# First batch in two token parts, and the first four tiles of a fused attention and FFN kernel as one written program order

## Chip, cores and metric

One core of a Trainium2 chip; the experiments ran in sessions on two such chips. The metric is device microseconds of the whole program, median of several executions; all runs quoted are of the state "fast" but for one, which is named. A profile is one of those executions. TensorE is PE in the profile (PEld its weight loads), VectorE is DVE, ScalarE is ACT, GpSimd is POOL.

## The reference

```python
# q, k, v: [8 batches, 8 heads, 576, 64] float32; w_in [512, 2048], w_out [2048, 512]
scores = q @ k.T / 8
rel = i - j
mask_plain = (rel >= 0) & (rel < 32)                       # heads 0 to 3
mask_dil   = (rel >= 0) & (rel < 128) & (rel % 4 == 0)     # heads 4 to 7
x = softmax(where(mask, scores, -1e9)) @ v                 # -> [4608 tokens, 512]
h = maximum(x @ w_in, 0)
out = (h * h) @ w_out
```

## The kernel before

Tokens come in 8 batches of 576 and the FFN takes them in 9 tiles of 512. Attention of a batch is cut into steps, each with a letter, a head pair e (0 and 1 plain, 2 and 3 dilated) and a token part: `q k` (capital for part 1) transpose on TensorE and copy out of PSUM, `v V` spread the values, `a b` are the scores of part 0 and 1, `o p` the value product, its normalization (two ScalarE passes, `rec`) and the product `xT` that the FFN reads. A tile's FFN is 32 groups of matmuls; a step has the number of the group (slot) behind which it is emitted. The order of emission is the order in which the instructions of each engine stand in its queue.

```python
FIRST = "k0 q2 q0 q3 k3 k2 k1 a0 b0 q1 a2 a1 v2 b2 b1 o0 p0 a3 o1 v3 p1 o2 b3 p2 o3 p3".split()
EARLY = {   # batch: "slot:step ..."
    1: ("21:q1 23:k0 23:q2 25:k2 25:v2 26:q0 27:v3 27:a0 27:a2 28:k1 29:k3 29:o0 29:a1 29:Q1 29:q3 29:o2  "
        "29:o1 30:a3 30:Q0 31:K1 31:o3 32:K0 32:Q2 34:Q3 35:b0 37:b1 37:K2 37:K3 37:V2 39:p0 39:b2 39:V3  "
        "39:p1 40:b3 43:p3 43:p2"),
    2: (...),                      # cut: "8:q0 ... 31:p3", counted from tile 1
}
WHOLE = (0, 2, 3)                  # batches that are transposed in one piece; 1 in two token parts
w_cuts = (0, 512, 1024, 2048)      # pieces of w_in
# ... cut: pools, masks, loads, steps
ps_f: 4 PSUM buffers, ps_a: 2, ps_o: 1, ps_d: 1
# value product of a part (cut)
for x, (oo, i, rh) in enumerate(mms):
    nc.tensor.matmul(oo, vb[:, e, i, :], rh, ...)           # po
for x, (dd, rh) in enumerate(dms):
    nc.tensor.matmul(dd, ones[:, :], rh, ...)               # pd, the row sums
nc.scalar.activation(rec[:, 0:n], d[:, 0:n], ACT.Ln)
nc.scalar.activation(rec[:, 0:n], rec[:, 0:n], ACT.Exp, scale=-1.0)
nc.vector.tensor_tensor(out=tok, in0=o, in1=rec, op=ALU.mult)   # xT
# the end of the kernel (cut)
for x, code in enumerate(FIRST):
    step(0, code)                                           # all of batch 0 ahead of the FFN
for tk0, nt in [(0, NT), (NT, NT // 2), (NT + NT // 2, NT // 2)] + [(NT * t, NT) for t in range(2, NTILES)]:
    groups += ffn_groups(tk0, nt)                           # tile 0 whole, tile 1 in halves
for g, group in enumerate(groups):
    group()
    while steps and steps[0][0] <= g:
        step(*steps.pop(0)[1:])
```

The softmax here doesn't subtract the row's maximum and nothing guards it: scores larger than these inputs give would overflow.

Of the kernel before, what the change touches and what calls it, by code (L numbers as in the profile page):

```python
# [12 lines left out]
RES = 4  # L13

ORDER = (0, 2, 1, 3)

FIRST = "k0 q2 q0 q3 k3 k2 k1 a0 b0 q1 a2 a1 v2 b2 b1 o0 p0 a3 o1 v3 p1 o2 b3 p2 o3 p3".split()

EARLY = {
    1: (  # L20
        "21:q1 23:k0 23:q2 25:k2 25:v2 26:q0 27:v3 27:a0 27:a2 28:k1 29:k3 29:o0 29:a1 29:Q1 29:q3 29:o2  "
        "29:o1 30:a3 30:Q0 31:K1 31:o3 32:K0 32:Q2 34:Q3 35:b0 37:b1 37:K2 37:K3 37:V2 39:p0 39:b2 39:V3  "
        "39:p1 40:b3 43:p3 43:p2"
    ),
    2: (
        "8:q0 10:k0 12:q2 13:k1 14:v3 14:a0 14:v2 15:q1 16:b0 16:o0 16:k2 18:q3 20:p0 21:a1 22:b1 22:k3 22:a2  "
        "22:o1 24:b2 25:o2 27:p1 27:a3 28:p2 28:b3 29:o3 31:p3"
    ),
}


def _masks() -> np.ndarray:
# [23 lines left out]
def kernel(  # L56
# [9 lines left out]
    nc = tc.nc  # L66
    P = nc.NUM_PARTITIONS
    B, H, S, D = q.shape
# [15 lines left out]
    MN = (64, M - 64)  # L84
    NT = 512
    NTILES = NTOK // NT
    WHOLE = (0, 2, 3)
    RING = 4 * S
    KT = DM // P
    NF = DFF // P  # L90
# [21 lines left out]
    mask_d = const.tile([P, 256 + 512], bf16, name="mask_d")  # L112
    mask_h = const.tile([P, 2 * 176 + 64], bf16, name="mask_h")

    w_cuts = (0, 512, 1024, 2048)
    w_in_sb = [
        const.tile([P, KT, c1 - c0], bf16, name=f"w_in{c0}") for c0, c1 in zip(w_cuts, w_cuts[1:])
    ]
# [94 lines left out]
    def trans(b: int, e: int, nm: str, part: int):  # L213

        ps = ps_a.tile([P, 1024], bf16, name="pa")
        t = staged(b, nm)
        copy = nc.scalar.copy if nm == "q" and e < NE // 2 else nc.vector.tensor_copy
        if b == 0:

            pv_ = ps[:, 0:S].rearrange("p (r m) -> p r m", r=RES)  # L220
            for r in range(RES):
                for a in range(2):
                    for hl in range(2):
                        nc.tensor.transpose(
                            pv_[64 * hl : 64 * hl + 64, r, 72 * a : 72 * a + 72],
                            t[0:72, 2 * e + hl, a, D * r : D * r + D],
                            ident[0:72, 0:72],
                        )
            if nm == "q":
                copy(qT[:, e, :, :], pv_)  # L230
                return
            for hl in range(2):
                rows = slice(64 * hl, 64 * hl + 64)
                if e < NE // 2:
                    copy(
                        kbd[rows, e, :, rows].rearrange("p i (m r) -> p i m r", r=RES),
                        pv_[rows, :, :].rearrange("p r (i m) -> p i m r", i=NB),
                    )
                else:
                    copy(  # L240
                        kbd[rows, e, 0:8, rows].rearrange("p (x r) m -> p r x m", x=2),
                        pv_[rows, :, 0:128].rearrange("p r (x m) -> p r x m", x=2),
                    )
                    copy(
                        kbd[rows, e, 8, rows].rearrange("p (m r) -> p m r", r=RES),
                        pv_[rows, :, 128:M].rearrange("p r m -> p m r"),
                    )
            return
        if b in WHOLE:
            m0, n, pitch, cuts = 0, M, M, [(t[0:72, :, a, :], 72 * a, 72) for a in range(2)]  # L250
        else:

            m0, n, pitch, cuts = MS[part], MN[part], 80, [(t[0:80, part, :, :], 0, 80)]
        pv_ = ps[:, 0 : 4 * pitch].rearrange("p (h c m) -> p h c m", h=2, c=2)
        for hl in range(2):
            for c in range(2):
                for src, c0, w in cuts:
                    nc.tensor.transpose(  # L258
                        pv_[:, hl, c, c0 : c0 + w], src[:, 2 * e + hl, P * c : P * c + P], ident[0:w, 0:w]
                    )  # L260
        halves(e, nm, pv_[:, :, :, 0:n], m0, n, copy)
# [31 lines left out]
    def blocks(b: int, e: int, part: int):  # L293



        if e < NE // 2:
            if part == 0:
                return [(i, None, 16 * i, min(16 * i + 24, 64)) for i in range(4)]
            return [(3, None, 64, 72)] + [(i, None, 16 * i, min(16 * i + 24, M)) for i in range(4, NB)]  # L300
        if b != 1:
            rs = (2 * part, 2 * part + 1)
            return [x for r in rs for x in ((r, r, 0, 96), (4 + r, r, 64, M))] + [(8, None, 128, M)] * (part == 0)
        if part == 0:
            return [(r, r, 0, 64) for r in range(RES)]
        return [x for r in range(RES) for x in ((r, r, 64, 96), (4 + r, r, 64, M))] + [(8, None, 128, M)]

    def half_at(b: int, e: int):

        return (352, mask_p) if e < NE // 2 else (256, mask_d) if b == 1 else (416, mask_h)  # L310

    pts = {}

# [25 lines left out]
    def pv(b: int, e: int, part: int, spare=None, name=""):  # L339
# [6 lines left out]
            o = spare.tile([P, 512], f32, name=name)  # L346
            d = spare.tile([P, 512], f32, name=name)
        c = half_at(b, e)[0] * part
        byr = dil and b != 1
        mms, dms = [], []  # L350
        if byr:
            n = 2 * M
# [39 lines left out]
        tok = xT[:, e, t0 : t0 + S]  # L392
        if byr:
            tok = tok[:, n * part : n * part + n]
        elif b == 1:
            tok = tok[:, RES * MS[part] : RES * MS[part] + n]
        else:
            tok = tok.rearrange("p (r m) -> p r m", r=RES)[:, :, MS[part] : MS[part] + MN[part]]
            o, rec = o3, rec[:, 0:n].rearrange("p (r m) -> p r m", r=RES)
# [4 lines left out]
    def step(b: int, code: str):  # L404
# [8 lines left out]
        elif what in "qQkK":  # L413
            trans(b, e, what.lower(), part)
        elif what in "vV":
            spread_v(b, e, [part] if b == 1 else [0, 1])
        elif what in "ab":
            scores(b, e, part, *((ps_f, "pf") if b == 0 else ()))
        elif b == 0 and part:
            pv(b, e, part, ps_a, "pa")  # L420
        elif b == 1 and e % 2:
            pv(b, e, part, ps_f, "pf")
        else:
            pv(b, e, part)
# [11 lines left out]
    def store(osb, pos: int):  # L436

        x = 0
        while x < P:
            b, y = divmod(pos + x, S)  # L440
            part = int(y >= RES * MN[0]) if b == 1 else 0
            w = MN[part] if b == 1 else M
            r, m = divmod(y - RES * MS[part], w)
            n = min(P - x, w - m)
            row = b * S + RES * (MS[part] + m) + r
# [95 lines left out]
    put(md[:, :, 32:112], mk[:, 160:240].unsqueeze(1).broadcast_to([P, RES, 80]))  # L541
    put(mask_d[:, 704:768], mk[:, 96:160])

    load_qk(0, None, [0])
    load_qk(0, None, [2, 3])
    load_qk(0, None, [1])
    load_v(0, [0, 1], "0pr1")

    for x, (w, c0, c1) in enumerate(zip(w_in_sb, w_cuts, w_cuts[1:])):
        nc.gpsimd.dma_start(w[:, :, :], moe_w_in[:, c0:c1].rearrange("(kt p) f -> p kt f", p=P))  # L550
    for c in range(4):
        nc.gpsimd.dma_start(
            w_out_sb[:, 4 * c : 4 * c + 4, :].rearrange("p f m -> p (f m)"),
            moe_w_out[512 * c : 512 * c + 512, :].rearrange("(p f) m -> p (f m)", p=P),
        )

    for x, code in enumerate(FIRST):
        step(0, code)
        if x == 1:

            for nm in "qk":
                nc.vector.memset(staged(1, nm)[64:80, 0, :, :], 0.0)
    zero_halves(vbd[1])
    load_qk(1, 0, [0, 1, 2, 3])
    load_v(1, [0])
    load_qk(1, 1, [0, 1, 2, 3])
    load_v(1, [1])
    load_qk(2, None, [0, 1, 2, 3])
    G = 2 * NF

    LOAD_V = {2: 0, 3: G + 16, **{b: G * (b - 2) for b in range(4, B)}}
    CROSS = {4: 2 * G + 8, **{b: G * (b - 2) + 5 for b in range(5, B)}}
    LOAD_QK = {3: G + 14, 4: 2 * G - 8, 5: 3 * G - 5, **{b: G * (b - 3) + 6 for b in range(6, B)}}
    groups, steps = [], []
    for tk0, nt in [(0, NT), (NT, NT // 2), (NT + NT // 2, NT // 2)] + [(NT * t, NT) for t in range(2, NTILES)]:
        groups += ffn_groups(tk0, nt)
    for b, table in EARLY.items():
        for x in table.split():
            slot, code = x.split(":")
            steps.append((G * (b - 1) + int(slot), b, code))  # L580
    steps += attention_steps(
        3, 2 * G, {"q": (-7, 8), "k": (-5, 8), "v": (-7, 8), "a": (-1, 8), "b": (0, 8), "o": (3, 8), "p": (6, 8)}
    )
    for b in range(4, B):
        steps += attention_steps(
            b, G * (b - 1),
            {"k": (-9, 4), "q": (-9, 4), "v": (-7, 8), "a": (-1, 8), "b": (0, 8), "o": (3, 8), "p": (6, 8)},
        )
    steps.sort(key=lambda x: x[0])
    for g, group in enumerate(groups):  # L590
        t = g // G
        for b in [x for x in CROSS if CROSS[x] == g]:
            for part in range(2):
                for nm in "kq":
                    cross(b, nm, part)
        for b in [x for x in range(2, B) if LOAD_V[x] == g]:
            load_v(b, [0, 1])
        for b in [x for x in range(3, B) if LOAD_QK[x] == g]:
            for part in [None] if b in WHOLE else [0, 1]:
                load_qk(b, part, [0, 1, 2, 3])  # L600
        group()
        while steps and steps[0][0] <= g:
            step(*steps.pop(0)[1:])

# [29 lines left out]
```

## Time and profile before

| | before |
|---|---|
| median of executions | 329.8 us |
| TensorE busy | 304.7 of 329.3 us |
| first w_in matmul, first w_out matmul | 27.1, 42.1 us |
| tile 0 done, tile 1 done, tile 2 done | 61.6, 105.6, 139.6 us |
| last FFN matmul done | 324.9 us |

Read it as a relay: from the first w_in matmul on, TensorE should never lack work, and a steady tile takes 32.5 us. What the first three tiles take over that is where time can come from. The stretches quoted in the prediction show it; "tile done" is the start of the next tile's first w_in matmul in the timeline.

### The profile page before, as it was taken

How to read it: one execution, taken by the hardware profiler on the slowest of the kernel's cores; microseconds unless marked ns; L12 is line 12 of the kernel's file. 1: busy time of each engine (PE TensorE's matmuls, PEld its weight loads, DVE VectorE, ACT ScalarE, POOL GpSimd, SP SyncE). 2: the span in 40 equal slices, each digit the busy share in tenths (PEclk: the TensorE clock that was granted, in tenths of full speed). 3: DMA queues.
4: the chain of work that ended last, by engine and by line, in shares of the span. 5: the costliest groups of instructions: out<-in, count | busy, mean ns of one | idle time of the engine just before them, and what ended most of it. 6: DMA issues, size and time to landing. Idle time of an engine off the chain costs nothing.

```text
span 329.3 us, 6594 instructions
## 1 busy us (share of the span) xinstructions
PE 304.7 (93%) x2490; PEld 184.0 (56%) x2490; DVE 199.6 (61%) x610; ACT 196.0 (60%) x419; POOL 82.3 (25%) x125
## 2 busy tenths in 40 slices
PE   0489998989997999999999999999999999999994
PEld 0474544775964655555559955555555555445541
DVE  6586518799865876898389738972897214203400
ACT  5096734776876893488448844884488446416511
POOL 8662287245235014440144024000000000000000
PEclk9997999999999999999999999999999999999999
DMA  7999999989976976999279927191200120031021
GB/s 98 126 174 214 202 168 129 182 98 159 129 77 87 148 93 91 155 152 170 55 115 148 171 60 116 34 146 32 71 27 3 43 79 7 1 94 35 0 64 64
DMA packets 74079, 33.07 MB, mean 100 GB/s; under 512 B 44736, under 2 KB 68416, under 8 KB 74048
## 3 DMA queue, kind: packets, MB, share of 16 engines
q0 software_dynamic: 49296, 18.37, 49.1%
q1 hardware_dynamic: 24608, 14.16, 19.3%
q8 instruction: 19, 0.31, 0.4%
q10 hardware_dynamic: 144, 0.13, 0.1%
q14 instruction: 12, 0.10, 0.1%
HBM read 36.83 MB, written 9.44 MB: 141 GB/s over the span
## 4 chain that ended last, share of the span: by engine, by line
PE 72%; DVE 12%; ACT 8%; DMA 3%; issue 2%; POOL 1%; ACTq 0%; POOLq 0%
PE pf L499 35%; PE pf L471 27%; DVE kbd L275 4%; PE po L385 3%; DMA kb<-in_k_dram 3%; PE pd L387 2%; DVE h2T L483 2%; DVE qT L271 2%; DVE xT L400 2%; ACT rec L389 1%; ACT h2T L482 1%; ACT qT L271 1%; ACT pt L333 1%; ACT osb L505 1%; PE pa L329 1%
## 5 line engine op out<-in xcount | busy, mean ns | idle before, releaser
L471 PE MATMUL pf<-xT,w_in 128*128 128x512 bf16 (+1 forms) x704 | 135.4, 342 | 0.3 <-ACT osb L505 0.2
L499 PE MATMUL pf<-w_out_sb,h2T 128*128 128x512 bf16 x576 | 134.8, 379 | 0.0
L482 ACT ACTIVATE h2T<-pf 128x512 bf16<-128x512 f32 x144 | 83.9, 596 | 29.6 <-PE pf L471 28.3
L471 PEld LDWEIGHTS <-w_in 128*128 128x128 bf16 x704 | 74.9, 114 | 40.3 <-issue 2.1
L483 DVE TENSOR_TENSOR h2T<-h2T 128x512 bf16<-128x512 bf16 x144 | 58.2, 422 | 40.3 <-ACT h2T L482 39.2
L499 PEld LDWEIGHTS <-h2T 128*128 128x128 bf16 x576 | 52.1, 98 | 53.4
L400 DVE TENSOR_TENSOR xT<-po,rec 128x288 bf16<-128x288 f32 (+2 forms) x56 | 25.5, 456 | 43.2 <-ACT rec L390 42.2
L505 ACT COPY osb<-pf 128x512 f32<-128x512 f32 x36 | 21.1, 587 | 49.5 <-PE pf L499 45.2
L170 POOL DMA_DIRECT2D vbd<-in_v_dram x36 | 25.9, 732 | 57.2 <-PE pd L387 43.8
L389 ACT ACTIVATE rec<-pd 128x288 f32<-128x288 f32 (+2 forms) x56 | 23.0, 411 | 25.9 <-PE pd L387 25.0
L333 ACT ACTIVATE pt<-pa 128x352 bf16<-128x352 f32 (+4 forms) x56 | 27.9, 501 | 5.9 <-PE pa L323 4.5
L390 ACT ACTIVATE rec<-rec 128x256 f32<-128x256 f32 (+2 forms) x64 | 28.4, 443 | 2.0
L385 PEld LDWEIGHTS <-vbd 128*128 128x128 bf16 x326 | 20.4, 100 | 15.9 <-issue 6.8
L385 PE MATMUL po<-pt,vbd 128*128 128x32 bf16 (+3 forms) x281 | 19.6, 200 | 4.4 <-DVE xT L400 4.3
L183 POOL DMA_DIRECT2D vd<-in_v_dram x28 | 17.0, 630 | 10.2 <-DMA kb<-in_k_dram 5.0
L387 PE MATMUL pd<-pt,mk 128*128 128x96 bf16 (+4 forms) x220 | 19.5, 211 | 0.0
L275 DVE COPY kbd<-pa 64x288 bf16<-64x288 bf16 (+2 forms) x32 | 12.8, 399 | 6.7 <-PE pa L258 6.1
L271 DVE COPY qT<-qx 64x288 bf16<-64x288 bf16 x64 | 15.5, 242 | 1.4
L387 PEld LDWEIGHTS <-mk 128*128 128x128 bf16 x252 | 15.2, 100 | 0.6 <-issue 0.5
L323 PEld LDWEIGHTS <-kbd 128*128 128x128 bf16 x176 | 11.6, 101 | 6.6 <-DVE qT L271 0.9
L275 DVE COPY kbd<-kx 64x288 bf16<-64x288 bf16 x32 | 15.0, 470 | 0.3
L334 DVE TENSOR_TENSOR pt<-pt,mask_p 128x352 bf16<-128x352 bf16 (+1 forms) x32 | 11.7, 372 | 5.3 <-ACT pt L333 5.2
(58 smaller groups left out, 210.3 us busy)
## 6 DMA issues: line engine op xcount, KB each, us to landing
vd<-in_v_dram POOLq DMA_DIRECT2D x32, 64.0 KB, 4.5
w_out_sb<-in_moe_w_out_dram POOLq DMA_DIRECT2D x4, 512.0 KB, 17.2
vbd<-in_v_dram POOLq DMA_DIRECT2D x28, 72.0 KB, 5.1
out_dram<-osb SPq DMA_DIRECT2D x7, 256.0 KB, 3.0
qb<-in_q_dram POOLq DMA_DIRECT2D x5, 320.0 KB, 5.9
kb<-in_k_dram POOLq DMA_DIRECT2D x5, 320.0 KB, 6.0
out_dram<-osb SPq DMA_DIRECT2D x7, 224.0 KB, 2.3
out_dram<-osb SPq DMA_DIRECT2D x12, 128.0 KB, 3.7
```

Of the source, the lines that this page charges most:

```text
L170: nc.gpsimd.dma_start(dst[rows, e, i0:i1, rows], v[b, 2 * e + hl, 64 * i0 : 64 * i1, :].rearrange("(i p) d -> p i d", p=64),)
L275: copy(kbd[rows, e, m0 // 16 : (m0 + n) // 16, rows].rearrange("p i (m c j) -> p j i m c", c=2, j=2)[:, jj, :, :, :], src.rearrange("p c ( ...
L333: nc.scalar.activation(pt[:, off : off + n], ps[:, 0:n], ACT.Exp, scale=SCALE)
L385: nc.tensor.matmul(oo, vb[:, e, i, :], rh, start=(x == 0), stop=(x == len(mms) - 1), skip_group_check=True)
L387: nc.tensor.matmul(dd, ones[:, :], rh, start=(x == 0), stop=(x == len(dms) - 1), skip_group_check=True)
L389: nc.scalar.activation(rec[:, 0:n], d[:, 0:n], ACT.Ln)
L390: nc.scalar.activation(rec[:, 0:n], rec[:, 0:n], ACT.Exp, scale=-1.0)
L400: nc.vector.tensor_tensor(out=tok, in0=o if o is o3 else o[:, 0:n], in1=rec if o is o3 else rec[:, 0:n], op=ALU.mult)
L471: nc.tensor.matmul(acc[u][:, nt * x + y0 : nt * x + y1], w_in_sb[piece][:, kt, c0 : c0 + 509 : 4], xT[:, kt, t0 : t0 + y1 - y0], start=(kt ...
L482: nc.scalar.activation(hv, acc[u][:, :].rearrange("p (x n) -> p x n", x=per), ACT.Relu)
L483: nc.vector.tensor_tensor(out=hv, in0=hv, in1=hv, op=ALU.mult)
L499: nc.tensor.matmul(cur[m][:, :], h2[:, f, P * m : P * m + P], w_out_sb[:, f, :], start=(f == 0), stop=(f == NF - 1),)
```

## The change

Its intent: the first half tile needs only 256 tokens, so batch 0 is loaded and computed in two token parts, FFN begins after part 0, and both halves of tile 0 use the first half of w_in before the second half is needed. For the first four tiles one written program gives the order of loads, steps and groups. (Not shown below: some steps of batch 0 use other PSUM buffers, and the q and k steps of batch 5 move into the program.)

```diff
-WHOLE = (0, 2, 3)
+WHOLE = (2, 3)
+PARTED = (0, 1)
-w_cuts = (0, 512, 1024, 2048)
+w_cuts = (0, 1024, 2048)
-FIRST = ...   EARLY = ...
+PROGRAM = (   # "|" is an FFN group; "L" is a load: batch, what, part, heads; i/o are pieces of w_in/w_out
+    "L0:q023 L0:q00 L0:q01 0k0 L0:q10123 0q0 0q1 0k1 L0:v0pd 0a0 0q2 L0:i0 0a1 0k3 L0:v1dpr 0k2 0q3 0Q1 "
+    "0K3 0a3 0Q3 0K2 0a2 0v2 0Q0 L0:i1 L0:o2 0K0 0o0 0v3 0b0 0Q2 0o2 0K1 0b3 0o1 L0:o0 0o3 0V3 0b2 0b1 | "
+    "0V2 | 0p0 | 0p1 0p2 | L0:o1 0p3 L0:o3 | | | y | | | | | | | | L1:q00123 z | | | | | L1:v0dp "
+    "L1:q10123 | | L2:qw0123 L1:v1dpr 1q1 1q3 | 1q2 | 1k2 | 1k1 1v3 | 1a2 | 1v2 1k0 1q0 | 1o2 | 1a0 1a1 | "
+    "1k3 1o0 1o1 | 1a3 1Q0 | 1K0 1o3 | 1Q1 1K1 | 1Q2 | 1b0 | | 1Q3 1K2 L2:vwpdr | | | 2q0 | | 2k0 1V2 | "
+    "1b2 1p0 | 1b1 1V3 1K3 | | 1p2 1p1 | 2a0 1b3 | 2k1 2o0 2b0 1p3 | 2q1 2k2 | | ..."
+    # cut: to the end of tile 3
+)
-for tk0, nt in [(0, NT), (NT, NT // 2), (NT + NT // 2, NT // 2)] + ...
+for tk0, nt in [(NT // 2 * t, NT // 2) for t in range(4)] + ...
+head = groups[:G]
+groups[:G] = [x for y in (0, 16, 4, 20, 8, 12, 24, 28) for x in head[y : y + 4]]
```

## The prediction

> **What bounds the kernel now.** I read the busy table first, then the table by stretches, then the chain that ended last, then the timeline of the places where the chain leaves TensorE.
>
> ```profile
> PE 304.7 (93%) x2490; PEld 184.0 (56%) x2490; DVE 199.6 (61%) x610; ACT 196.0 (60%) x419; POOL 82.3 (25%) x125
> ...
> PEclk9997999999999999999999999999999999999999
> ```
>
> TensorE is busy 93%, at full clock but for one slice, the fourth. So the end is TensorE's work plus the time in which it lacked work. Cutting the span where one FFN tile of 512 tokens gives way to the next (the copies of the last output rows in the chain, and the first matmul of the next tile) shows where it lacked work:
>
> ```profile
> 0.00:27.20 27.20, 13.33 (x239) 11.98 (x240) 18.26 (x38) 14.55 (x37) 17.89 (x30) 0.97 1.11 140
> 27.20:61.60 34.40, 32.84 (x216) 16.92 (x213) 19.52 (x56) 19.19 (x47) 16.49 (x24) 0.97 1.24 179
> 61.60:105.50 43.90, 40.13 (x487) 30.89 (x483) 35.24 (x116) 30.96 (x71) 18.66 (x27) 1.00 0.98 118
> 105.50:139.60 34.10, 34.05 (x292) 19.38 (x290) 25.16 (x84) 22.36 (x50) 10.11 (x16) 1.00 0.84 119
> 139.60:172.10 32.50, 32.30 (x244) 17.88 (x241) 23.27 (x77) 21.15 (x45) 9.39 (x15) 1.00 0.89 124
> 172.10:204.70 32.60, 32.41 (x307) 24.59 (x304) 23.26 (x77) 21.14 (x46) 9.37 (x15) 1.00 0.92 125
> ```
>
> Columns after the stretch and its length: PE, PEld, DVE, ACT and POOL busy, clock, DMA share, GB/s. Rows are the start and tiles 0 to 4. The steady tile is 32.5 us. FFN work in one tile is 128 matmuls of 512 columns; the chain shows 64 of them in 13.81 us, so 27.6 us, which leaves 4.9 us for one batch's attention. Tile 2 takes 1.6 us more because its batch is also transposed on TensorE. Tile 1 takes 43.9 us. The start takes 27.2 us, and the first matmuls after it run at half clock:
>
> ```profile
> 26.77 0.48 PE pa L387 x3
> 27.25 4.50 PE pf L471 x16
> 31.78 10.52 PE pf L471 x48
> 42.30 5.18 PE pf L499 x24
> ```
>
> Sixteen matmuls cost 4.50 us there and 3.5 us at the rate of the next 48 (0.22 us each), so about 1.0 us is lost to the clock. Where tile 1 loses time:
>
> ```profile
> 100.28 0.33 PE L385 MATMUL po<-pt,vbd 128*128 128x96 bf16 x5 [0.69 <-DVE xT L400]
> 100.44 1.99 DVE L275 COPY kbd<-pa 64x288 bf16<-64x288 bf16 x4
> 102.46 0.46 DVE L400 TENSOR_TENSOR xT<-po,rec 128x288 bf16<-128x288 f32 x1
> 102.97 0.33 PE L385 MATMUL po<-pt,vbd 128*128 128x96 bf16 x5 [1.15 <-DVE xT L400]
> ```
>
> TensorE waits for an output normalization (xT) that stands behind four key copies of a later batch on VectorE, which was busy 35.24 of 43.9 us in this tile.
>
> **What the Trainium skill says.** *TensorE: Matmul & The Clock Gate*, "Part 1: The HAM clock gate": about 3.4 us of sustained work release a half-rate clock. The trace agrees in kind: granted clock 0.50 from 26 to 28 us, 0.69 from 28 to 30, then 1.00. An earlier FFN does not escape this, since the work before it stays sparse. The same page, "Architectural detail", calls ScalarE and VectorE strict FIFOs; the timeline above agrees, with the xT instruction behind the four copies. *DMA: Bandwidth & Descriptors*, "Specifications", asks for at least 512 B per transfer; from 12 to 14 us, 1557 of 1617 packets are below that and 112 GB/s move, against 211 GB/s for weights from 30 to 32 us. *Perfetto Trace Analysis*, "Tensor Engine Instruction", calls matmul ends estimated. So I count from start to start (512 columns: 216 ns, where the table of groups says 379).
>
> **The change, part by part.**
>
> *Two token parts for batch 0.* TensorE gets its transposes as 128 pieces of 64 or 80 tokens instead of 128 of 72: no gain or loss. What moves is the dependency. The first half tile (256 tokens) needs only part 0 of batch 0, so the four PV steps of part 1 go behind the first FFN groups. Now the start, by hand. In the trace about 1.15 MB of q and k are in by about 12 us, and part 1 of k is last in the new order too, so it lands at 12. From there VectorE has, in the order of the built program up to the last xT of part 0: four k copies for each of the two dilated pairs at part 1 (0.96 us a pair, from 0.27 and 0.21 us), two k copies for each plain pair (0.9), three q or mask items of about 0.3 early and three of about 0.4 late, two value spreads of 0.6, and four xT of 0.42. Sum: 1.9 + 1.8 + 0.9 + 1.2 + 1.2 + 1.7 = 8.7 us. With 0.8 us from landing to the first copy it ends near 21.5. ScalarE has about 6 us in the same stretch, so VectorE sets it. I allow 0.5 for gaps: FFN starts at 22.0 instead of 27.25, **5.2 us earlier**.
>
> *Do weights allow this?* The first 1 MB piece of w_in (two pieces of 512 KB in the old kernel, the second landed at 24.9) now stands behind 1.15 MB of q/k and 0.26 MB of v, not all 0.58 MB. Its eight-deep ring lets it be issued at about 12 instead of 15.5 us. After v part 0 at about 14.5 it needs 5 us (205 KB/us, from landings at 24.9, 29.9, 32.3 and so on): 19.5 us, just ahead. The second piece lands at about 27, needed at about 32. The w_out pieces end at 37 instead of 39.8, needed at 40.
>
> *What is given back.* Four PV steps now cost TensorE 1.8 us inside the FFN (12 matmuls of 37 ns a plain step, double at half clock). The second half waits about 0.6 us for the last of their xT (a PV step, two ScalarE passes of 0.4 us and the xT of 0.5 are a chain of 1.5 us; one group of 0.44 and a PV step cover the rest). Sixty-four more matmuls at 256 columns cost 110 x 2 - 216 = 4 ns each, 0.26 us. The clock costs perhaps 0.5 us more. Sum 3.2. So mm1 of tile 0 ends near 40.3, against 42.3: **net 2.0 us gained** at the start.
>
> *Weights by pieces.* Both halves use piece one before piece two is wanted; the time is already in the line above.
>
> *One program for tiles 0 to 3.* Tile 0's second GEMM: the old tile took 34.4 us, of which FFN is 27.6, clock 1.0 and the batch 1 part about 4, so about 1.7 us of stalls. Batch 1 now lands about 2.5 us earlier; I expect 1.0 us of stalls, **0.7 gained**. Tile 1: 43.9 minus 27.9 of FFN, minus 3.4 for the rest of batch 1 and 7.0 for batch 2 with its transposes, is about **5.5 us of stalls**. The built order moves most early transposes of batch 3 (old slots 57 to 63) behind tile 1 and spreads the parts of batch 1 over slots 32 to 47, so xT no longer stands behind that run of copies. VectorE is left with some 33 us of work in a tile of 38.4 us, still 85%, so I keep 2.5 us of stalls: **3.0 gained**. Tiles 2 and 3 had no measurable stalls before; the last PV of batch 2 now comes one group later, beside the tile that needs it: **0.5 lost**. Later tiles are unchanged.
>
> Sum: 2.0 + 0.7 + 3.0 - 0.5 = 5.2 us, which gives 324.8. I choose 324.3, a little lower, because a schedule as fine as this was presumably tuned and the tile 1 term could reach 4 or 5.
>
> **Rivals.**
>
> (a) *The FFN begins earlier but starves.* Part 1's values are loaded behind the first weight piece. If they or the second weight piece land late, TensorE stalls at p0 or at the fifth group and the 2.0 vanishes: 326.5. For it: DMA share is over 1.1 in this stretch. Against: 0.32 MB of small packets behind 19.5 us should land by 22 to 23, p0 is wanted at about 25.5.
>
> (b) *Tile 1 is VectorE's.* If about 36 us of VectorE work with its waits is the true bound there, the new order cannot take out more than 1 us: 326.5. For it: 35.24 of 43.9 us busy. Against: tile 4 runs with 23.3 of 32.6 at no loss, and the stalls seen are single FIFO waits.
>
> (c) *Loss-free program.* All stalls go, except about 1.5 us: another 2.5 us gained, 321.8.
>
> (d) *The finer order backfires*, as with output stores blocking ScalarE (4.3 us of waits of the output copy on stores before): 329 to 331.
>
> **Range and chances.** The start time is uncertain by 1.5 us, tile 1 by 2 us, the rest by 1 us; in squares 2.7 us, so 8 in 10 gives about 3.4 us to each side, less below since loss-free is a floor: 321.0 to 327.5. The 2% line is 330.0 x 0.98 = 323.4, just below my middle. I give faster by over 2% 0.41, same 0.56, slower 0.03.
>
> **What would show it.** First FFN matmul (w_in) at 21 to 24 us, with granted clock near 0.5 around it; first w_out matmul at 39 to 41.5; tile 0 done at about 58.5 to 60; tile 1 at about 98 to 101, with VectorE still over 80% there; tile 2 in 34 to 35; steady tile 32.5 as before. It is wrong if the FFN waits for w_in or for v part 1 by over a microsecond, if tile 1 stays at 42 us or more, or if a later tile departs from 32.5.

## The result

The changed kernel takes 321.8 us (321.46 to 322.35), against 329.8 (328.77 to 331.06) before, in runs of the same rounds. The ratio is 0.9757, 95% interval 0.972 to 0.9795: faster by 2.4%. The two profiled executions, 331.1 and 322.4 us, are at the slow end of their kernels' fast runs, so the traces differ by 8.7 us where the medians differ by 8.0. A ratio is the mean of one kernel's fast runs over that of the other's in the same rounds, so not quite the ratio of the medians. The predicted time was 324.3 us with a range of 321.0 to 327.5, so the range held and the forecast gain of 5.5 us was 8 us.

The page of the changed kernel:

```profile
PE 303.8 (95%) x2564; PEld 190.3 (59%) x2564; DVE 203.1 (63%) x624; ACT 195.9 (61%) x421; POOL 84.2 (26%) x130
```

TensorE has the same work (303.8 us busy against 304.7), in a span of 320.6 instead of 329.3 us. So the gain is lost time taken out. The stretches by tile of the changed kernel, same columns as in the prediction (start, then tiles 0 to 4):

```profile
0.00:21.90 21.90, 11.82 (x200) 9.53 (x201) 15.16 (x40) 11.17 (x30) 15.10 (x28) 1.00 1.07 135
21.90:58.40 36.50, 34.90 (x326) 25.65 (x324) 23.51 (x69) 21.48 (x52) 15.86 (x24) 1.00 1.17 183
58.40:97.40 39.00, 38.75 (x480) 30.44 (x477) 34.90 (x114) 30.07 (x71) 18.60 (x27) 1.00 1.01 119
97.40:131.90 34.50, 34.46 (x300) 20.02 (x299) 28.91 (x90) 24.98 (x55) 12.70 (x19) 1.00 0.81 120
131.90:164.00 32.10, 32.10 (x241) 17.88 (x239) 23.84 (x77) 20.77 (x44) 12.24 (x20) 1.00 1.13 149
164.00:196.60 32.60, 32.60 (x306) 24.74 (x304) 22.31 (x75) 21.34 (x45) 9.70 (x15) 1.00 0.87 125
```

Tile 1 fell from 43.9 to 39.0 us, with TensorE busy in 38.75 of them, while VectorE's work there is nearly the same (34.90 against 35.24 us). TensorE's idle time in tile 1 fell from 3.8 us (43.90 less 40.13 busy) to 0.25; the other 1.4 us are TensorE work that is shorter or stands in another tile. Tile 0 with its first half overlapping attention takes 36.5 us from its start, 2.0 more than before, but it starts 5.2 us sooner. From the starts of the first matmul of each kind, to the hundredth:

| stretch | before | after | gained | predicted |
|---|---|---|---|---|
| up to the first w_in matmul | 27.09 | 21.94 | 5.2 | 5.2 |
| first GEMM of tile 0, with the value steps inside | 15.05 | 19.12 | -4.1 | -3.2 |
| second GEMM of tile 0 | 19.47 | 17.36 | 2.1 | 0.7 |
| tile 1 | 43.96 | 39.01 | 4.95 | 3.0 |
| tile 2 | 34.04 | 34.35 | -0.3 | -0.5 |
| tiles 3 and 4 | 65.04 | 64.30 | 0.7 | 0 |
| sum | | | 8.6 | 5.2 |

The last FFN matmul is done at 316.29 against 324.85 us, the same 8.6. The chain that ended last shows the first GEMM:

```profile
22.13 3.75 PE pf L475 x24
...
30.50 3.54 PE pf L475 x31
34.07 7.15 PE pf L475 x64
41.22 5.18 PE pf L503 x24
```

L475 is the w_in matmul, L503 the w_out one. The first 24, of 256 columns, take 3.75 us where 24 of the later ones take 2.7 (7.15 over 64 is 0.112 each). The trace says why: its matmuls start 0.213 us apart up to 24.1 us and 0.109 apart from 24.3 us on, and its first record of the clock, full rate, stands at 24.26 us. (The column in the table above reads 1.00 before that only because there is no record yet.) Between 25.7 and 30.5 us stand the four value steps; in the timeline they wait, as the brackets say (idle time, and what ended it):

```profile
27.87 0.43 PE L389 MATMUL po<-pt,vbd 128*128 128x32 bf16 x9 [0.66 <-DVE xT L404]
29.68 0.38 PE L391 MATMUL pa<-pt,mk 128*128 128x320 bf16 x3 [0.43 <-DVE xT L404]
30.50 10.72 PE L475 MATMUL pf<-xT,w_in 128*128 128x256 bf16 x95 [0.33 <-DVE xT L404]
```

That is 1.4 us of waiting for xT. In the rest of tiles 0 and 1 the waits of TensorE nearly vanish. The view of waits from 38 to 106 us, before (total us, times, longest):

```profile
PE po L385 <- DVE xT L400: 1.8, 2, 1.2
PE pa L258 <- ACT pt L333: 1.1, 2, 0.8
PE pa L258 <- DVE kbd L282: 0.7, 1, 0.7
PE pa L329 <- ACT pt L333: 0.6, 1, 0.6
PE pa L323 <- ACT qT L271: 0.3, 1, 0.3
PE pf L471 <- ACT osb L505: 0.2, 1, 0.2
PE pa L323 <- DVE qT L271: 0.2, 1, 0.2
```

and after:

```profile
PE pf L475 <- ACT osb L509: 0.2, 1, 0.2
PE pa L262 <- ACT qT L275: 0.2, 1, 0.2
```

They sum to 4.9 us before and 0.4 after. The two stretches gained 7.1 us together; the list has only waits that the view attributes, and the work in tile 1 differs a little, since the last value step of batch 2 (`2p3`, slot 64) moved into tile 2.

### The profile page after: what moved, and what is told of

Same layout as the page of the kernel before. It is cut to its first block, busy times and chain, and to the rows that moved or that the text cites. A ratio compares the mean times of both kernels' runs of the same rounds, so it can differ in the third digit from the quotient of the medians.

```text
span 320.6 us, 6759 instructions
## 1 busy us (share of the span) xinstructions
PE 303.8 (95%) x2564; PEld 190.3 (59%) x2564; DVE 203.1 (63%) x624; ACT 195.9 (61%) x421; POOL 84.2 (26%) x130
## 4 chain that ended last, share of the span: by engine, by line
PE 87%; DVE 5%; ACT 3%; issue 1%; DMA 1%; POOL 1%; ACTq 0%; POOLq 0%
PE pf L503 38%; PE pf L475 35%; PE po L389 3%; PE pd L391 3%; PE pa L262 2%; PE pa L327 2%; PE pa L333 2%; PE pa L230 1%; DVE kbd L279 1%; DMA kb<-in_k_dram 1%; DVE h2T L487 1%; ACT osb L509 1%; DVE xT L404 1%; ACT rec L393 1%; ACT qT L275 1%
## 5 line engine op out<-in xcount | busy, mean ns | idle before, releaser
L475 PE MATMUL pf<-xT,w_in 128*128 128x256 bf16 (+1 forms) x768 | 135.8, 328 | 0.6 <-DVE xT L404 0.3
L503 PE MATMUL pf<-w_out_sb,h2T 128*128 128x512 bf16 x576 | 135.1, 379 | 0.0
L475 PEld LDWEIGHTS <-w_in 128*128 128x128 bf16 x768 | 82.0, 114 | 35.2 <-issue 1.2
L503 PEld LDWEIGHTS <-h2T 128*128 128x128 bf16 x576 | 52.1, 98 | 53.0
L509 ACT COPY osb<-pf 128x512 f32<-128x512 f32 x36 | 21.1, 585 | 44.1 <-PE pf L503 44.1
L176 POOL DMA_DIRECT2D vbd<-in_v_dram x40 | 28.2, 726 | 45.9 <-PE pd L391 35.7
L337 ACT ACTIVATE pt<-pa 128x352 bf16<-128x352 f32 (+4 forms) x60 | 29.9, 506 | 8.5 <-PE pa L333 4.3
L389 PEld LDWEIGHTS <-vbd 128*128 128x128 bf16 x332 | 19.7, 99 | 10.9 <-issue 2.1
L391 PE MATMUL pd<-pt,mk 128*128 128x96 bf16 (+6 forms) x220 | 19.4, 209 | 0.0
L159 POOL DMA_DIRECT2D qb<-in_q_dram x14 | 10.1, 722 | 27.9 <-PE po L389 24.6
L189 POOL DMA_DIRECT2D vd<-in_v_dram x24 | 14.7, 650 | 5.8 <-DMA kb<-in_k_dram 5.8
L195 POOL DMA_DIRECT2D vbd<-in_v_dram x16 | 9.7, 617 | 19.9 <-PE pd L391 5.3
L391 PEld LDWEIGHTS <-mk 128*128 128x128 bf16 x248 | 14.5, 99 | 0.7 <-issue 0.5
```

The source lines that it names most:

```text
L176: nc.gpsimd.dma_start(dst[rows, e, i0:i1, rows], v[b, 2 * e + hl, 64 * i0 : 64 * i1, :].rearrange("(i p) d -> p i d", p=64),)
L337: nc.scalar.activation(pt[:, off : off + n], ps[:, 0:n], ACT.Exp, scale=SCALE)
L389: nc.tensor.matmul(oo, vb[:, e, i, :], rh, start=(x == 0), stop=(x == len(mms) - 1), skip_group_check=True)
L391: nc.tensor.matmul(dd, ones[:, :], rh, start=(x == 0), stop=(x == len(dms) - 1), skip_group_check=True)
L475: nc.tensor.matmul(acc[u][:, nt * x + y0 : nt * x + y1], w_in_sb[piece][:, kt, c0 : c0 + 509 : 4], xT[:, kt, t0 : t0 + y1 - y0], start=(kt ...
L503: nc.tensor.matmul(cur[m][:, :], h2[:, f, P * m : P * m + P], w_out_sb[:, f, :], start=(f == 0), stop=(f == NF - 1),)
```

## The experiments

Three questions: is it the start or the order; which part of the order; and what of the start is still lost. Edits are to the changed kernel unless said otherwise. Times of different sessions are compared through their ratios to the kernel before. That kernel spreads: its 35 fast runs in the experiments' sessions go from 328.8 to 332.0 us, and the 13 with a mean clock of 0.995 are 1.1 us longer on average than the 22 with more. So ratios that rest on four runs have intervals of about 0.4% to each side, and a difference of 1 us between two variants lies inside them. The stretches in the traces are far steadier: tile 1 takes 39.01 to 39.04 us in all eight profiled runs that leave its steps, and batch 1's in tile 0, in the new order.

### The start alone

```diff
 # start, halves of tile 0 and first loads of the changed kernel; from slot 14 on:
-    program entries for batches 1 to 5
+    EARLY, attention_steps and the load slots of the kernel before
```

> The changed kernel's start (batch 0 in two parts, interleaved halves of tile 0, its loads) with the step slots and loads that the kernel before had for batches 1 to 7. In the two traces the changed kernel is ahead by 5.3 us at the first FFN matmul, 1.1 us at the first w_out matmul, 3.2 us at the end of tile 0 and 8.1 us at the end of tile 1. Theory: the start is worth only what is left at the first w_out matmul, and the rest comes from the order of the steps: 1 to 2 us faster than before, 328 us, tile 1 still 43 to 44 us long. Rival: the start, through data that lands earlier, is what frees tile 0's second half and tile 1 too: 5 us or more faster, tile 1 at 41 us or less.

It gave a wrong result (relative error 0.10) and 341.7 us: batch 2's values were loaded into the buffer that batch 0's last value steps still had to read. The fault was in my edit and it says nothing on the change. Mended (batch 2's values loaded at slot 5 instead of 0):

> As e1_start_only, which was wrong by my edit: it loaded batch 2's values ahead of the last value steps of batch 0, which now run among the first FFN groups and share that buffer. Here they are loaded after them. The run with the order alone has shown tile 0's second half (17.37 us) and tile 1 (39.0 us) as in the changed kernel, with the old start. Theory now: the start alone is worth at most 1 us: 329 us, second half of tile 0 near 19.5 and tile 1 near 44 us as before. Rival: the start helps the old order by 3 us or more, 327 or less.

Measured: 328.9 us, ratio 0.9966 (0.995 to 0.9982, 16 runs). First w_in matmul at 21.4, first w_out matmul at 39.8, second GEMM of tile 0 19.46 us, tile 1 43.99 us. In this trace the start is 2.4 us ahead at the w_out matmul, yet over 16 runs the kernel is 0.3%, 1.1 us, faster; 1.0 us of the 2.4 is the slow clock, which the trace of before met in its first GEMM (15.05 us against 14.02 in the next run) and this one did not. The second GEMM and tile 1 are as long as before, and the view of waits from 38 to 106 us is that of before, line for line. So an earlier start does not shorten the stretches of the old order, and by itself it is worth about one microsecond.

### The order alone

```diff
 # the kernel before; from slot 14 on:
-    EARLY, attention_steps, loads of batches 1 and later
+    the changed kernel's program entries
```

> The start of the kernel before (batch 0 whole, tile 0 in 512 columns) with the changed kernel's slots and loads from slot 14 on. Theory: the order carries most of the gain by itself: 6 to 7 us faster than before, about 323.5 us, tile 1 at 39 to 40 us. Rival: the order needs the earlier landing of the changed start, for it puts part 1 of batch 1's values behind all of batch 2's q and k: then stalls on landings appear and the gain is under 3 us, 327 us or more.

Measured: 323.1 us (322.3 to 324.46), ratio 0.9784 (0.9745 to 0.9823). First w_in matmul at 26.4, first w_out at 40.4, second GEMM 17.37 us, tile 1 39.04 us. The table by stretches, second GEMM and tile 1:

```profile
40.37:57.74 17.37, 17.21 (x147) 9.39 (x146) 9.89 (x38) 8.66 (x25) 8.08 (x11) 1.00 1.33 177
57.74:96.78 39.04, 38.79 (x479) 30.43 (x477) 34.91 (x114) 30.12 (x71) 18.63 (x27) 1.00 0.98 114
```

With the old start the two stretches are as short as in the changed kernel: the order carries 2.2 of the 2.4% (1.8 to 2.6 by the interval). "Order" here takes in the loads from slot 14 on; the two runs below that put old steps back, with the loads of batches 1 and 2 untouched, tell the two apart. The rival, that the order needs the earlier data, falls. The profiled execution ran its first GEMM in 14.0 us, with no slow matmuls, and so reached w_out 0.7 us before the changed kernel did in its first profile; in the run of before the same start took 15.05.

### The split of the start undone

```diff
-... 0b2 0b1 | 0V2 | 0p0 | 0p1 0p2 | L0:o1 0p3 L0:o3 |
+... 0b2 0b1 0V2 0p0 0p1 0p2 0p3 | | | | L0:o1 L0:o3 |
```

> The changed kernel with the part 1 value steps of batch 0 all ahead of the first FFN group: only the split of the start is undone. Theory: the early FFN start is nearly all given back, since in the changed kernel the four steps cost 1.9 us of TensorE and 1.4 us of waits among the first FFN groups: FFN starts 3 to 4 us later, near 25.5 us, the first w_out matmul at 41 to 41.5 against 41.1, total within 0.5 us of the changed kernel, 321.5 to 322.5. Rival: the split is the gain of the start: w_out starts at 43 or later and the total is 2 us longer or more, 324.

Measured: 323.3 us (323.08 to 324.14), ratio 0.9791. The changed kernel's two sessions gave 0.9757 and 0.9751, so this is 0.4%, 1.2 us, longer, between what theory and rival said. First w_in matmul at 26.7 instead of 21.9, first w_out at 41.75 against 41.06 and 40.42 in the two profiles of the changed kernel. Of 4.8 us of earlier start, about one reaches the end. Part of that one may be the clock: this trace has a record of half clock from 24.7 to 28.1 us, over the first 1.4 us of FFN, and its w_in matmuls take 14.98 us where the run with fillers below, with none slow, takes 14.48. All four of its runs have a mean clock of 0.995, the nine of the changed kernel 0.998 or more.

### Batch 3's first copies put back into tile 1

```diff
-slot 65: 3k0 3k2    slot 70: 3q0 3v2
+slot 57: 3q0        slot 59: 3k0        slot 65: 3k2        slot 70: 3v2
```

> The changed kernel with batch 3's first q and k transposes and copies put back in tile 1, at the old slots 57 and 59, nothing else. Theory: output normalizations of batch 2 stand behind the key copies on VectorE as before, and TensorE waits for the single PSUM buffer of the value product: 1.5 to 2.5 us longer than the changed kernel, about 324, with waits of 0.5 to 1.2 us on xT near the end of tile 1. Rival: tile 1 gained from the spread of batch 1's steps and VectorE has room for these: within 0.5 us, 322.

The edit puts back more than it says. The changed kernel has two steps of batch 3 in tile 1, `3k1 3q1` at slot 62, as many as the kernel before had (q0 and k0 at slots 57 and 59); they stay, so tile 1 now holds four.

Measured: 323.0 us (322.78 to 323.99), ratio 0.9784, so 0.9 to 1.1 us over the changed kernel. Tile 1 takes 40.9 us, 1.9 more, and tile 2 34.06, 0.3 less. Of the 1.9 us, 0.7 is TensorE's time for the 16 transposes of the two steps (4.13 against 3.45 us for all of the tile's), which in the changed kernel are done in tile 2, and 1.1 is idle time (1.3 against 0.25). The size in tile 1 is as expected, but the kind of wait is not. The view of waits from 38 to 106 us:

```profile
PE pa L333 <- ACT qT L275: 0.8, 1, 0.8
PE po L389 <- DVE xT L404: 0.2, 1, 0.2
```

The longer wait is a score that waits for a q copy on ScalarE; the wait for xT is only 0.2 us. Here the added steps made TensorE wait more for ScalarE than for VectorE; both copy its results out of PSUM.

### Batch 1's part 0 in the old order

```diff
-1q1 1q3 | 1q2 | 1k2 | 1k1 1v3 | 1a2 | 1v2 1k0 1q0 | 1o2 | 1a0 1a1 | 1k3 1o0 1o1 | 1a3 1Q0 | 1K0 1o3 | 1Q1 1K1
+1q1 | | 1k0 1q2 | | 1k2 1v2 | 1q0 | 1v3 1a0 1a2 | 1k1 | 1k3 1o0 1a1 1Q1 1q3 1o2 1o1 | 1a3 1Q0 | 1K1 1o3 | 1K0
```

> The changed kernel with the part 0 steps of batch 1 (slots 21 to 32 in tile 0) in the old order. Theory: these steps are what shortened the second half of tile 0 from 19.5 to 17.4 us, so it is 19 to 19.5 us again and the total 1.5 to 2 us longer than the changed kernel, 323.5. Rival: the second half gains from data that lands sooner or from the rest of the program: under 0.5 us, 322.

Measured: 323.6 us (323.2 to 323.68), ratio 0.9785, 0.9 to 1.1 us over the changed kernel. The second GEMM of tile 0 is 19.46 us again, to 0.01 us that of before, and tile 1 stays at 38.9. So these steps are the 2.1 us of that stretch; the loads of batch 1 were not touched. Waits of before are back in the view from 38 to 106 us:

```profile
PE pa L263 <- DVE kbd L287: 0.7, 1, 0.7
PE pa L263 <- ACT pt L338: 0.3, 1, 0.3
```

The ratio shows only half of the 2.1 us, but it cannot tell 1 us from 2. The times themselves, 323.2 to 323.7 against 321.4 to 322.4 us in the two sessions of the changed kernel, differ by 1.8. The two profiles differ by 0.9 (spans of 321.4 and 320.6), since this one reached w_out 1.1 us sooner: its clock went to full rate at 22.2 us and that of the changed kernel's first profile at 24.3.

### Batch 1's part 1 and batch 2 at the old slots, batch 3 as in the changed kernel

```diff
-slots 32 to 64: 1Q1 1K1 | 1Q2 | 1b0 | | 1Q3 1K2 | | | 2q0 | | 2k0 1V2 | 1b2 1p0 | ... 2p3
+slots 32 to 63: 1Q1 1K1 1Q2 | | 1Q3 | 1b0 | | 1b1 1K2 1K3 1V2 | | 1p0 1b2 1V3 1p1 | 1b3 2q0 | ... 2p3   (as EARLY)
 # batch 3 as in the changed kernel, its loads moved to slots 46 and 50
```

> The changed kernel with the part 1 steps of batch 1 and all steps of batch 2 at their old slots in tile 1, but batch 3's first copies kept out of it. Putting those back (e4_b3_early) made tile 1 1.9 us longer (40.9 against 39.0 us), out of the 4.9 that tile 1 gained. Theory: the other 3 us are the order of these steps: tile 1 at 41.5 to 42.5 us, total 2.5 to 3 us longer, 324.5. Rival: one key is enough, the copies out of the tile, and the rest of the order is worth under 1 us: tile 1 at 40 us or less, total 322.5.

Measured: 326.3 us (325.88 to 326.83), ratio 0.9869, 3.7 to 3.9 us over the changed kernel. Tile 1 takes 44.1 us, as long as before, though batch 3 begins at slot 62 with two steps, as in the changed kernel, and not at slot 57. (So its copies are later in the tile, not out of it as the expectation says.) The waits from 38 to 106 us:

```profile
PE pa L262 <- ACT qT L275: 1.3, 2, 1.1
PE po L389 <- DVE xT L404: 1.0, 2, 0.5
PE pa L262 <- ACT pt L337: 0.9, 1, 0.9
PE pa L333 <- ACT pt L337: 0.6, 1, 0.6
```

The two waits for xT that the prediction showed (0.69 and 1.15 us) are 0.54 and 0.44 now, so the place of the copies was part of them; but one wait of 1.12 us came from my putting `Q1 K1 Q2` into one slot, which the old kernel did not do. Even with that taken off, tile 1 is near 43 (an estimate, 44.1 less 1.1). So the later place of batch 3 brings at most about 1 us by itself, and the order of the other steps brings most of tile 1's gain.

### The clock at the start

```diff
+    def filler(n):
+        t = ps_d.tile([P, 512], f32, name="pd")
+        for _ in range(n):
+            nc.tensor.matmul(t[:, :], ones, mk[:, :], start=True, stop=True)
+    filler(8)        # ahead of the first step, and one behind each of the early steps
```

> The changed kernel with useless matmuls on constants ahead of the first transposes and between the early steps of batch 0 (24 of 512 columns in all, into a PSUM tile that nothing reads). In the changed kernel's trace the first 24 w_in matmuls take 3.75 us where 24 at 110 ns are 2.64, and the matmuls before them run near half rate, though the granted clock column reads 1.00 there. Theory: TensorE starts at half clock and the column does not show it; work from 3 us on lifts it, so that the 24 take about 2.7 us, the early steps get shorter and the kernel ends 1 to 1.5 us sooner than the changed one. Rival: the slow matmuls wait for operands or weight loads: the 24 still take 3.7 us and the end is the same or later by the filler's cost.

Measured: four fast runs of 321.62 to 322.99 us, ratio 0.9767, in the same rounds as the changed kernel's 0.9751: no gain. A fifth run, 327.26 us, was in the slow state and is left out. From the timeline, the first filler and the first long run of w_in matmuls:

```profile
2.96 3.60 PE L608 MATMUL pd<-mk 128*128 128x512 bf16 x8 [2.96 <-DMA mk<-mask_patterns]
...
23.86 2.56 PE L475 MATMUL pf<-xT,w_in 128*128 128x256 bf16 x22 [0.31 <-DVE xT L404]
```

Eight matmuls of 512 columns on constants that are already there, waiting for nothing, take 3.60 us with the modelled end of the last; from start to start they are 427 ns apart. The steady rate is 216. The table by stretches of this run says of that time:

```profile
4.00:6.00 2.00, 2.00 (x6) 0.61 (x4) 1.67 (x2) 1.83 (x9) 2.00 (x4) 1.00 1.06 127
```

The column before the last two is the granted clock, 1.00. So it does not show the slow clock that the kernel starts with. The clock records in the trace explain it: they begin with a record of full rate at 12.35 us, nothing stands before it, and where there is no record the column reads 1.00. From 12.4 us on the matmuls in this run are short, and the 22 w_in matmuls next to each other start 0.109 us apart (2.40 us to the next start in the chain). The half of the theory that concerns the clock holds; the half that concerns the gain does not: the filler itself stands in front of the transposes, the first w_in matmul comes at 23.2 instead of 21.9 us, and the first w_out at 41.6.

The same records explain most of the spread of the start. Full rate comes at 24.26 us in the first profile of the changed kernel, at 22.88 in the second, at 22.19 and 23.86 in two of the runs above, and the w_in matmuls of the first GEMM take 15.46, 14.75, 14.58 and 15.35 us: the later the record, the longer, with nothing changed in the program there.

### A transfer taken out of the way

```diff
-L0:i0 0a1 0k3 L0:v1dpr ... L0:i1
+L0:i0 0a1 0k3 L0:v1dp L0:i1 L0:v1r ...
```

> The changed kernel with one load moved: the second piece of w_in is issued ahead of the two last small value loads of batch 0. In the changed kernel's trace the DMA engines move only 14 to 55 GB/s from 21 to 24 us, since the eighth load behind the first piece of w_in waits for that piece to land. Theory: the transfer is hidden anyway: the pieces land 3 to 4 us sooner (second piece near 27 instead of 30.5 us), and the end moves by less than 0.5 us. Rival: batch 1's steps in the second half of tile 0 are held by data: the end comes 1 to 3 us sooner.

In the changed kernel only eight loads are under way at a time: each is issued after the eighth before it has landed. The eighth behind the first piece of w_in is a small one. GpSimd's timeline shows it waiting for that piece, while only six small loads, landed by 22.7 us, are still under way:

```profile
21.15 0.61 POOL L195 DMA_DIRECT2D vbd<-in_v_dram  x1 [3.59 <-DMA w_in<-in_moe_w_in_dram]
```

From 21 to 24 us the last two columns of the table by stretches, DMA share and GB/s, in the changed kernel and then in this run:

```profile
21.00:24.00 3.00, 3.00 (x28) 2.26 (x26) 2.76 (x8) 2.35 (x6) 2.85 (x5) 1.00 0.41 30
21.00:24.00 3.00, 2.83 (x34) 2.67 (x33) 2.75 (x9) 2.18 (x6) 2.63 (x5) 1.00 1.16 210
```

The second piece of w_in landed by 28.1 instead of 30.5 us. The total is 322.4 us (321.59 to 323.06), ratio 0.977 against 0.9751: no gain, as the transfer is hidden. The second GEMM of tile 0 takes 17.38 us, unchanged, so data for batch 1 that lands sooner changes nothing. The edit has a price: the value step p2 waits 1.1 us for the small load that now stands behind the big one. This profile also met a record of half clock from 28.5 to 31.9 us, so its first w_out matmul, at 41.8, says nothing on the loads.

### Half a tile first

```diff
-groups[:G] = [x for y in (0, 16, 4, 20, 8, 12, 24, 28) for x in head[y : y + 4]]
+groups[:G] = [x for y in (0, 4, 16, 20, 8, 12, 24, 28) for x in head[y : y + 4]]
-| 0V2 | 0p0 | 0p1 0p2 | L0:o1 0p3 L0:o3 |
+| 0V2 | 0p0 | 0p1 | 0p2 L0:o1 L0:o3 | 0p3 |       (and the load order of the last experiment)
```

> The load order of e6_ring, and the first half of tile 0 goes through all of its first GEMM before the second half begins; the four part 1 value steps of batch 0 are spread over groups 1 to 4 of it. Theory: the three waits of TensorE for xT in the changed kernel (0.66, 0.43 and 0.33 us) are a chain of value step, two ScalarE passes and a multiplication with too little FFN beside it; four more groups beside it hide them, and the end is 1 to 1.4 us sooner than the changed kernel. Rival: the waits come back at the second half's first groups or as a wait for the second piece of w_in: no gain.

Measured: 320.9 us (319.9 to 321.88), ratio 0.9718 (0.968 to 0.9757), against 0.9751 for the changed kernel in the same rounds. The waits for xT from 20 to 45 us are 0.2 us in all instead of 1.4, there is no wait for the load, and the first w_out matmul starts at 39.6 instead of 40.4 us. The gain is 0.8 us of median, a little under what was expected; the ranges and intervals of the two overlap, so it is likely but small.

The changed kernel again, in the same rounds: 321.7 us (321.45 to 322.24).

> The changed kernel itself on the same chip, so that the others are compared with it: 0.976 of the time before.

### What sets the start of the FFN

```diff
-copy = nc.scalar.copy if nm == "q" and e < NE // 2 else nc.vector.tensor_copy
+copy = nc.scalar.copy if nm == "q" and (e < NE // 2 or b == 0) else nc.vector.tensor_copy   (on top of half a tile first)
```

> e7_half_first with the copies of batch 0's dilated q (four of 0.3 to 0.4 us) on ScalarE instead of VectorE. The prediction took VectorE's 8.7 us after the landing of k as what sets the FFN's start. Theory: with 0.7 us less of it in that stretch the first w_in matmul comes 0.5 to 0.7 us sooner, and the end about as much, 320.3. Rival: ScalarE, which carries the passes for the normalizations in the same stretch, takes over: the start moves by less than 0.2 us or later.

Measured: 321.0 us (320.64 to 321.24), ratio 0.9706, against 0.9718 for its base: the same. The first w_in matmul starts at 22.45 against 22.58 us. From 12 to 22.5 us VectorE's work fell from 8.03 to 7.15 us and ScalarE's rose from 5.29 to 6.56. The rival's figure is right: taking that from VectorE does not move the start by as much. So VectorE's sum of work alone does not set the start; what does was not shown.

## Why the prediction was right, and where its sizes were off

**The start.** The prediction had the FFN begin at 22.0 us, and it began at 21.94. The sum on VectorE that led there did not prove to be the reason: moving 0.9 us of it away moved the start by 0.13. What was given back was put at 3.2 us and was 4.1. From start to start in the trace, the value steps took 2.2 us instead of 1.8, the waits for xT 1.4 instead of 0.6, and the halved matmuls about 0.5 instead of 0.26 (14.48 us in the run with fillers against 13.98 with the order alone, neither with slow matmuls). The further 0.5 us for the clock did not come: before and after lost about 1.0 us each to slow matmuls in their first GEMM. The sign that the prediction named, a granted clock near 0.5, did not stand in the column for want of a record; the matmuls were at half rate until 24.3 us all the same. So the net gain at the first w_out matmul is 1.1 instead of 2.0 us in these traces. The runs of the start alone (1.1 us faster over 16 runs) and of the split undone (1.2 us longer, with the clock in it) agree.

**Weights.** They were in time, as predicted, though not for the times given: the second piece landed by 30.5 rather than 27 and the last of w_out at 41.3 rather than 37, since the ring of eight loads, which the prediction used to argue for an early issue, also stopped the queue behind the first piece. The second piece was not needed before 34, and the run with the transfer moved showed that it was hidden. Rival (a), that the FFN starves, is refuted.

**The second GEMM of tile 0.** The term said 0.7 us of 1.7 us of stalls gained, through data that lands sooner. It is 2.1 us, of which 1.4 is idle time of TensorE, and the reason named was wrong: the order of batch 1's steps alone takes it away and gives it back (19.46 and 17.4 us), with data sooner or later.

**Tile 1.** The mechanism (order, not VectorE's amount of work) was right, and rival (b) is refuted: 34.90 us of VectorE work fit into 39.0 us. The size was too small: 3.0 us predicted, 4.95 measured. The term that was mis-sized is "VectorE is left with some 33 us of work in a tile of 38.4 us, still 85%, so I keep 2.5 us of stalls". There were almost none; 0.25 us of idle time is left in tile 1. The 5.5 us of stalls that it started from were too many as well: its own table has TensorE idle for 3.8 us there (43.9 less 40.13), and the rest of the gain is TensorE's work, 1.4 us less. The cause given, key copies of batch 3 in front of xT, is only a part, and the order was read wrongly: two steps of batch 3 stand in tile 1 before and after, only later, at slot 62 instead of 57 and 59. With that place and the other steps old, tile 1 stays at 44.1 us.

**Tiles 2 to 4.** Tile 2 lost 0.3 (0.5 predicted). Tiles 3 and 4 gained 0.7 us together, which the prediction left at nothing. It comes with the order: they take 64.3 us with the order alone and 65.0 with the start alone. The view of waits has 0.4 us of waits for xT in them before and none after; the other 0.3 us stay open.

Rival (c), a program free of loss at 321.8 us, is what came: 321.81. That it agrees to 0.01 us is luck, since the start gave 0.9 us less than predicted, and tiles 3 and 4 gave 0.7 us that it left at nothing. The prediction gave this rival too little weight, for it read a busy share of 85% as a reason for stalls; it also held "the same" likelier (0.56) than faster by over 2% (0.41), which came.

## What to carry to other kernels

Where a bound engine is fed by in-order helpers, measure what the stalls of a stretch are worth, and do not take a busy helper as proof that they must stay: here a good order took nearly all of them with a helper busy for 89% of the stretch, and the order of the steps was worth 2.2 of 2.4%. An earlier start of the bound engine is worth only what remains after the work pushed behind it and its waits: here one of five microseconds. Before a transfer is moved, look at whether anything waits for it.

## What the Trainium skill lacked or had wrong

- *TensorE: Matmul & The Clock Gate*, "Part 1: The HAM clock gate", says that about 3.4 us of sustained work release the clock. In the run with the filler TensorE had eight matmuls in a row from 2.96 us and then fillers and transposes in turn, with pauses of 0.2 us in all from 4 to 12 us. Its 512-column matmuls still started 427 ns apart at the end of the eight, and the first record of full rate is at 12.35 us, 9.4 us after the first filler. So 3.4 us of such work did not release it here; which part of the mix does not count is not shown.
- The same section warns that trace events of the clock can be unreliable. Here they were not: in the changed kernel the first record of full rate, at 24.26 us, stands where the starts of equal matmuls go from 213 to 109 ns apart, and in the filler run, at 12.35 us, where those of equal transposes go from 53 to 29 ns.
- The same section does not say that nothing is recorded before the first change. In these traces the clock column then reads 1.00 (to 24.26 us in the changed kernel) while TensorE is at half rate; the rate has to be read from starts of equal matmuls (512 columns: 216 ns when fast, 427 at the start).
- *DMA: Bandwidth & Descriptors*: no page that I read says that a queue whose loads each wait for the eighth before them can run nearly empty behind one large load. Here it fell to 30 GB/s from 21 to 24 us, against 210 with one load moved.
